# Reordering the work of the two mixing slots in a fused attention and spectral-mix kernel

## The chip, the cores and the metric

The kernel runs on one core of a Trainium2 chip. The metric is the device time of one execution in microseconds (us). The kernel before took 959.21 us (median of 3 runs, 957.13 to 961.86).

## The reference

Soft-capped attention over 8 batches, 12 heads, 448 positions and head size 64 gives x; a mixing layer works on it:

```
scores = cap * tanh((q @ k.T / 8) / cap)
x      = softmax(scores) @ v                     # heads joined: 448 x 768 per batch
theta  = x @ w_theta
y      = w_tok_r @ (x * cos(theta)) + w_tok_i @ (x * sin(theta))
u      = x + y
out    = u + max(u @ w_ch, 0)
```

All arrays are float32. The kernel computes the mixing products from two rounded parts of each operand, a high one and a low one, with three matmuls per product (high by high, low by high, high by low).

## The kernel before, in words

The work is cut into 48 slots (`slot`, and `opening` for the first eight), one for each pair of heads. A slot s computes the scores of its pair in two halves (words SA and SB of the scripts below, PE line L214), their tanh (ACT L216) and exponential (A and B, ACT L222), and for the pair before it the product with v (V, PE L254), its copy out of PSUM (x, ACT L260) and the row sums of the exponentials by matmuls with ones (r, PE L273). From slot 8 on each slot also carries a sixth of one batch's mixing layer. The six parts of a batch are: three blocks of theta (th0 to th2), three more (th3 to th5), three blocks of the token mixing (mix0 to mix2), three more (mix3 to mix5), and twice three blocks of the channel product (ch). A part's matmuls fill most of PE's slot: 54 for three th or ch, 63 for three mix. "The first mixing slot" is below the one with mix0 to mix2, "the second" the one with mix3 to mix5.

Between th and mix each of the six blocks j passes through these steps, by their words in the scripts:

- fold (DVE L344 to L346): theta is brought into one turn; sincos (ACT L350, L351): the sine and cosine of three blocks at once, with a load of ACT's table before it and another before the next tanh.
- rotate (DVE L355) and turn: a transpose within 32 by 32 squares (DVE L362), then a store of 448 KB to a scratch buffer in DRAM (SP queue, L364).
- back: four DMAs that read the block back in its other order (SP queue, L370). They wait until the store has landed.
- high (ACT L378) and low (DVE L384): the two rounded parts, zh and zl. Each of the two tiles has two buffers, so that high2 and low2 wait until mix0 is done, high5 and low5 until mix3 is done.
- mix (PE L392 to L394), gain (DVE L398, which adds the result to x and frees its PSUM buffer), us (ACT L318 and DVE L319, the parts of u), ch, and the evacuation of ch (DVE L406).

Nothing reorders this work: each engine and each DMA queue does its instructions in the order in which the scripts name the steps. `part_scripts` has one script for each of the six parts, `TAIL` the scripts of the last slots, in which no attention is left (batch 7, and the last part of batch 6). The SP queue carries also the loads of q and k (word q, L182: slot s loads for slot s+2 into a buffer that prep, DVE L192 and L193, must have read before), the four DMAs that spread the reciprocal row sums (inv: DVE L300, then L304), the output stores (L407) and the weight loads (L107). The loads of v go through ACT's queue (L186).

The weights are split into high and low parts on the chip (`Split`) at the places listed in `WEIGHTS`: ">" loads a block, "*" scales it on ACT (L111) and "#" on DVE (L114), and the bare name does the split, five to six instructions on DVE (L119 to L128); where `act` is true the rounding among them is ACT's (L124). Channel blocks ch2 to ch5 are loaded and split in slots 10 to 13, beside the mixing of batch 0. Even blocks use one staging buffer and odd ones another, the same two (`g_sb`) that hold the angles of blocks 0 to 2 and 3 to 5.

PSUM accumulators come from a pool of four buffers in turn. A matmul group can start only when its buffer's last reader is done: the copy x, the reciprocal, the gain or L406.

## Time and profile before

| | before |
|---|---|
| time, median of 3 runs | 959.21 us |
| the profiled execution's own time | 966.61 us |
| its span, from the first to the last instruction | 964.8 us |
| PE busy | 924.9 us (96%) |
| DVE busy | 688.4 us (71%) |
| ACT busy | 588.8 us (61%) |
| mean granted TensorE clock over the span | 0.983 |

Durations below come from the profiled execution. The ends of matmuls are modelled, so a row of busy PE hides nothing but also says little; the number to read is the distance from one matmul's start to the next one's, and windows that are cut at the start of a group of matmuls give it.

### The profile page before, as it was taken

The page shows a single profiled execution, that of the slowest core. Times are in us where ns is not written, and L with a number is a line of the kernel's source. Part 1 is how long each engine was busy: PE and PEld are TensorE (multiplying, and loading weights), DVE is VectorE, ACT ScalarE, POOL GpSimd, SP SyncE. Part 2 cuts the span into 40 slices and gives each one's busy share as a digit, 9 for nine tenths or more (in the row PEclk, how much of TensorE's full clock was granted, in tenths as well). Part 3 has the DMA queues.
Part 4 walks back from the last instruction along what each step waited for, and adds up shares of the span by engine and source line. Part 5 has one row for each costly group of instructions (what it writes and reads, how often), then busy time and mean ns, then how long its engine had stood idle before and what let it go on. Part 6 is the DMA issues. An engine that isn't in the chain of part 4 may idle for free. (4 is left out here: it accounts for less than half of the span.)

```text
span 964.8 us, 12481 instructions
## 1 busy us (share of the span) xinstructions
PE 924.9 (96%) x4888; PEld 668.0 (69%) x4888; DVE 688.4 (71%) x877; ACT 588.8 (61%) x561; POOL 0.4 (0%) x6
## 2 busy tenths in 40 slices
PE   8999988989989999999998999899999999999797
PEld 4334656657767787677676767676876677789697
DVE  5998975887876578666777568775787568775641
ACT  6988864467844687555956469445874568644220
POOL 0000000000000000000000000000000000000000
PEclk9999989999999999999999999999999999999899
DMA  7674155422552235432542324622254333411701
GB/s 242 198 222 116 61 148 158 144 80 72 156 163 77 75 106 149 113 112 68 153 144 62 102 67 144 181 67 77 83 156 134 86 96 119 149 38 49 238 2 60
DMA packets 65154, 112.64 MB, mean 117 GB/s; under 512 B 8128, under 2 KB 44992, under 8 KB 65088
## 3 DMA queue, kind: packets, MB, share of 16 engines
q1 hardware_dynamic: 60096, 102.82, 35.4%
q10 hardware_dynamic: 4992, 8.95, 3.2%
q8 instruction: 40, 0.66, 0.3%
q14 instruction: 26, 0.21, 0.1%
HBM read 67.70 MB, written 33.03 MB: 104 GB/s over the span
## 5 line engine op out<-in xcount | busy, mean ns | idle before, releaser
L216 ACT ACTIVATE p<-s,qscale 112x1792 f32<-112x1792 f32 x96 | 168.5, 1755 | 140.1 <-PE s L214 139.9
L222 ACT ACTIVATE p<-p,cap_sb 112x1792 f32<-112x1792 f32 x96 | 169.4, 1785 | 0.4
L254 PE MATMUL a<-p,v 112*64 112x448 f32 x768 | 154.9, 545 | 0.0
L392 PE MATMUL mx<-wtk_h,zh 128*128 128x448 f32 x336 | 128.5, 383 | 12.7 <-ACT zh L378 12.7
L394 PE MATMUL mx<-wtk_h,zl 128*128 128x448 f32 x336 | 127.5, 380 | 8.3 <-DVE zl L384 8.2
L393 PE MATMUL mx<-wtk_l,zh 128*128 128x448 f32 x336 | 126.1, 375 | 0.0
L254 PEld LDWEIGHTS a<-p,v 112*64 112x64 f32 x768 | 50.8, 136 | 86.9 <-issue 76.8
L327 PE MATMUL ch<-us,wch_h 128*128 128x448 f32 x288 | 107.1, 372 | 0.0
L327 PE MATMUL th<-xs,wth_h 128*128 128x448 f32 x288 | 106.9, 371 | 0.0
L328 PE MATMUL ch<-us,wch_h 128*128 128x448 f32 x288 | 105.4, 366 | 0.0
L328 PE MATMUL th<-xs,wth_h 128*128 128x448 f32 x288 | 105.3, 366 | 0.0
L329 PE MATMUL ch<-us,wch_l 128*128 128x448 f32 x288 | 105.3, 366 | 0.0
L329 PE MATMUL th<-xs,wth_l 128*128 128x448 f32 x288 | 105.3, 366 | 0.0
L384 DVE TENSOR_TENSOR zl<-g_sb,zh 128x896 fp32r<-128x896 f32 x48 | 51.9, 1083 | 70.7 <-ACT zh L378 70.5
L247 DVE TENSOR_TENSOR ps<-ps,p 112x896 f32<-112x896 f32 x80 | 87.1, 1089 | 1.4
L392 PEld LDWEIGHTS mx<-wtk_h,zh 128*128 128x128 f32 x336 | 65.5, 195 | 26.2 <-ACT zh L378 14.9
L378 ACT CAST zh<-g_sb 128x896 fp32r<-128x896 f32 x48 | 44.9, 937 | 63.2 <-DMA g_sb<-turn 31.4
L300 DVE RECIPROCAL ri<-r 128x448 f32<-128x448 f32 x24 | 70.6, 2944 | 16.6 <-PE r L273 16.6
L394 PEld LDWEIGHTS mx<-wtk_h,zl 128*128 128x128 f32 x336 | 65.4, 195 | 18.0 <-DVE zl L384 12.3
L393 PEld LDWEIGHTS mx<-wtk_l,zh 128*128 128x128 f32 x336 | 65.5, 195 | 5.5
L406 DVE SCALAR_TENSOR_TENSOR x<-ch,x 128x448 f32<-128x448 f32 x48 | 29.6, 619 | 50.2 <-PE ch L329 50.2
L327 PEld LDWEIGHTS ch<-us,wch_h 128*128 128x128 f32 x288 | 54.2, 188 | 10.3 <-issue 2.7
(73 smaller groups left out, 1338.5 us busy)
## 6 DMA issues: line engine op xcount, KB each, us to landing
turn<-g_sb SPq DMA_DIRECT2D x48, 448.0 KB, 2.8
g_sb<-turn SPq DMA_DIRECT2D x192, 112.0 KB, 3.2
qk_sb<-in_qk SPq DMA_DIRECT2D x35, 448.0 KB, 3.9
bc<-ri SPq DMA_DIRECT2D x96, 112.0 KB, 2.3
out_dram<-x SPq DMA_DIRECT2D x48, 224.0 KB, 2.0
v<-in_v ACTq DMA_DIRECT2D x39, 224.0 KB, 2.6
qk<-in_qk SPq DMA_DIRECT2D x13, 448.0 KB, 3.5
g_sb<-in_wth SPq DMA_DIRECT2D x6, 768.0 KB, 5.3
```

The source lines that it names most:

```text
L216: return lambda: nc.scalar.activation(pp, sp[:CP, :, :, :S], AF.Tanh, scale=qscale[:CP])
L222: nc.scalar.activation(pp, pp, AF.Exp, scale=cap_sb[:CP])
L247: nc.vector.tensor_tensor(pst[k], pst[k], pt[k, 1][:, i], op=ALU.add)
L254: nc.tensor.matmul(acc[hh * D : (hh + 1) * D, :S], va[:, hh, c, :], pt[k, c // 2][:, c % 2, hh, :], start=c == 0, stop=c == NCH - 1)
L300: nc.vector.reciprocal(ri, r[:, :S])
L327: nc.tensor.matmul(acc[:, :S], wh[:, j, ms], t[:, 0, :], start=j == 0, stop=False)
L328: nc.tensor.matmul(acc[:, :S], wh[:, j, ms], t[:, 1, :], start=False, stop=False)
L329: nc.tensor.matmul(acc[:, :S], wl[:, j, ms], t[:, 0, :], start=False, stop=j == NJ - 1)
L384: nc.vector.tensor_tensor(zl.rearrange("p c (g t) -> p c g t", g=4), turned(j), zh.bitcast(F32).rearrange("p c (g t) -> p c g t", g=4), op ...
L392: nc.tensor.matmul(acc[:, :S], zh[:, c, :], wtk_h[:, c, :], start=c == 0, stop=False)
L393: nc.tensor.matmul(acc[:, :S], zh[:, c, :], wtk_l[:, c, :], start=False, stop=False)
L394: nc.tensor.matmul(acc[:, :S], zl[:, c, :], wtk_h[:, c, :], start=False, stop=c == NC2 - 1)
```

## The change

Four scripts and the weight list are written in another order; no computation is added or dropped. In the first mixing slot: high1 moves ahead of the sines, low0 and low1 follow at once on DVE, the load q moves from behind the fourth back to just behind prep, rotate5, turn5 and back5 move in from the second mixing slot, back4 and back5 now stand ahead of inv (whose four DMAs go out on the same queue), and gain1 moves in from the second slot. In the slot before it, b (DVE L247, the sum over the second half of the exponentials) moves ahead of fold5. In the tail high0, low0, high1 and low1 move from behind the three ch blocks to around the second sincos. In the weight list ch4 is scaled and rounded on DVE instead of ACT, and the load of ch3 is issued ahead of the split of ch2, where it stood behind the load of ch4.

```diff
-            steps["ch", m] = Split(room_g(m), w_ch[m], wch_h[:, :, ms], wch_l[:, :, ms], m != 2)
+            steps["ch", m] = Split(room_g(m), w_ch[m], wch_h[:, :, ms], wch_l[:, :, ms], m not in (2, 4))
...
-        (8, "b"): "tk5", (8, "c"): "*tk6 *ch1", (9, "a"): "tk6 ch1", (10, "c"): ">ch2", (11, "c"): "#ch2 ch2 >ch4 >ch3", (12, "b"): "*ch3 ch3 >ch5", (12, "c"): "*ch4 ch4", (13, "b"): "*ch5 ch5",
+        (8, "b"): "tk5", (8, "c"): "*tk6 *ch1", (9, "a"): "tk6 ch1", (10, "c"): ">ch2", (11, "c"): ">ch3 #ch2 ch2 >ch4", (12, "b"): "*ch3 ch3 >ch5", (12, "c"): "#ch4 ch4", (13, "b"): "*ch5 ch5",
...
-            " A th3 fold3 a B th4 fold4 back2 wc th5 fold5 b",
-            "SA high0 sincos1 low0 V wa x v r high1 low1 SB tB prep wb rotate3 turn3 high2 mix0 gain0 low2 rotate4 turn4 back3 inv A"
-            " back4 q B wc mix1 mix2",
-            "SA gain1 a- gain2 rotate5 turn5 high3 low3 V wa x v r high4 low4 SB tB prep b- back5 q wb A mix3 a high5 low5 gain3 us0"
+            " A th3 fold3 a B th4 fold4 back2 wc th5 b fold5",
+            "SA high0 low0 high1 sincos1 low1 V wa x v r SB tB prep q wb rotate3 turn3 high2 rotate4 turn4 back3 mix0 gain0 low2"
+            " rotate5 turn5 back4 back5 inv A B wc mix1 gain1 mix2",
+            "SA a- gain2 high3 low3 V wa x v r high4 low4 SB tB prep b- q wb A mix3 a high5 low5 gain3 us0"
...
-        "rotate0 turn0 rotate1 turn1 back0 rotate2 turn2 back1 th3 fold3 th4 fold4 back2 th5 fold5 sincos1 rotate3 turn3 rotate4 turn4"
+        "rotate0 turn0 rotate1 turn1 back0 rotate2 turn2 back1 th3 fold3 th4 fold4 back2 th5 fold5 high0 low0 sincos1 high1 low1 rotate3 turn3 rotate4 turn4"
...
-        "high0 low0 high1 low1 mix0 high2 low2 gain0 us0 mix1 high3 low3 gain1 us1 mix2 high4 low4 gain2 us2",
+        "mix0 high2 low2 gain0 us0 mix1 high3 low3 gain1 us1 mix2 high4 low4 gain2 us2",
```

The SP queue in the two mixing slots of batch 2, from the return of block 2 on, before (turn_j is block j's scratch buffer, bc a spread reciprocal):

```order
L370 DMA g_sb_87<-turn_2_2532 32x4x224 x4
L364 DMA turn_3_2685<-g_sb_88 128x896
L364 DMA turn_4_2716<-g_sb_88 128x896
L370 DMA g_sb_88<-turn_3_2685 32x4x224 x4
L304 DMA bc_2724<-ri_2722 64x448 x2
L304 DMA bc_2727<-ri_2722 64x448 x2
L370 DMA g_sb_88<-turn_4_2716 32x4x224 x4
L182 DMA qk_sb<-in_qk 128x896
L364 DMA turn_5_2802<-g_sb_88 128x896
L370 DMA g_sb_88<-turn_5_2802 32x4x224 x4
L182 DMA qk_sb<-in_qk 128x896
```

The same stretch of the SP queue after the change:

```order
L370 DMA g_sb_87<-turn_2_2532 32x4x224 x4
L182 DMA qk_sb<-in_qk 128x896
L364 DMA turn_3_2686<-g_sb_88 128x896
L364 DMA turn_4_2692<-g_sb_88 128x896
L370 DMA g_sb_88<-turn_3_2686 32x4x224 x4
L364 DMA turn_5_2725<-g_sb_88 128x896
L370 DMA g_sb_88<-turn_4_2692 32x4x224 x4
L370 DMA g_sb_88<-turn_5_2725 32x4x224 x4
L304 DMA bc_2737<-ri_2735 64x448 x2
L304 DMA bc_2740<-ri_2735 64x448 x2
L182 DMA qk_sb<-in_qk 128x896
```

The store and the return of block 5 now stand ahead of the reciprocals' DMAs, and no load of q and k stands directly ahead of that store; one stands directly ahead of block 3's store instead.

DVE in the first mixing slot of batch 1 before (zl_j is the low part of block j, mx_j a mixing result, the pair L355 and L362 a rotate and its transpose):

```order
L384 TENSOR_TENSOR zl_1_1779<-g_sb_87,zh_1_1777 128x896
L192 CAST hi_1796<-qk_sb 128x896
L193 TENSOR_TENSOR lo_1797<-qk_sb,hi_1796 128x896
L355 TENSOR_TENSOR g_sb_88<-g_sb_88,x_915 128x896
L362 STREAM_TRANSPOSE g_sb_88<-g_sb_88 128x896
L398 TENSOR_TENSOR x_564<-mx_0_1806,x_564 128x448
L384 TENSOR_TENSOR zl_2_1829<-g_sb_87,zh_2_1804 128x896
L355 TENSOR_TENSOR g_sb_88<-g_sb_88,x_1063 128x896
L362 STREAM_TRANSPOSE g_sb_88<-g_sb_88 128x896
L300 RECIPROCAL ri_1839<-r_1772 128x448
L398 TENSOR_TENSOR x_628<-mx_1_1854,x_628 128x448
```

DVE at the same place after the change:

```order
L384 TENSOR_TENSOR zl_1_1761<-g_sb_87,zh_1_1757 128x896
L192 CAST hi_1796<-qk_sb 128x896
L193 TENSOR_TENSOR lo_1797<-qk_sb,hi_1796 128x896
L355 TENSOR_TENSOR g_sb_88<-g_sb_88,x_919 128x896
L362 STREAM_TRANSPOSE g_sb_88<-g_sb_88 128x896
L355 TENSOR_TENSOR g_sb_88<-g_sb_88,x_1067 128x896
L362 STREAM_TRANSPOSE g_sb_88<-g_sb_88 128x896
L398 TENSOR_TENSOR x_564<-mx_0_1815,x_564 128x448
L384 TENSOR_TENSOR zl_2_1838<-g_sb_87,zh_2_1805 128x896
L355 TENSOR_TENSOR g_sb_88<-g_sb_88,x_1200 128x896
L362 STREAM_TRANSPOSE g_sb_88<-g_sb_88 128x896
L300 RECIPROCAL ri_1852<-r_1776 128x448
```

The second rotate and transpose stand ahead of zl_2, and the third pair has come in ahead of the reciprocal.

## Rows read from the trace of the kernel before

**Rows 1.** The page, its first line on the engines: busy time, share of the span, instructions.

```profile
PE 924.9 (96%) x4888; PEld 668.0 (69%) x4888; DVE 688.4 (71%) x877; ACT 588.8 (61%) x561; POOL 0.4 (0%) x6
```

**Rows 2.** What PE waited for over the whole span: line waited for, us in total, times, the longest.

```profile
PE mx L392 <- ACT zh L378: 12.7, 6, 2.9
PE s L214 <- ACT p L216: 9.2, 9, 4.2
PE mx L394 <- DVE zl L384: 8.2, 8, 5.4
```

**Rows 3.** Windows over the 63 matmuls of the second mixing slot, each from the first matmul's start to the start of the group behind it, for batches 0, 2 and 6, and the sum over the seven windows of batches 0 to 6: length, busy us of PE, PEld, DVE, ACT and POOL with instructions, granted TensorE clock (PEclk), busy share of the DMA engines, GB/s.

```profile
151.59:169.64 18.05, 14.99 (x66) 12.62 (x64) 10.57 (x13) 8.30 (x8) 0.00 (x0) 0.91 0.47 148
...
388.55:404.06 15.51, 13.59 (x67) 11.60 (x65) 11.09 (x13) 8.30 (x8) 0.00 (x0) 1.00 0.46 140
...
842.94:855.99 13.05, 13.05 (x66) 11.76 (x64) 10.17 (x13) 8.31 (x8) 0.00 (x0) 1.00 0.24 76
sum 116.79, PE 101.17 PEld 85.91 DVE 80.55 ACT 58.11 POOL 0.00; mean PE 14.45 PEld 12.27 DVE 11.51 ACT 8.30 POOL 0.00
```

**Rows 4.** The timeline of PE in batch 2: the first matmul of mix0, and the first of mix5 with the idle time ahead of it and what ended that. Columns: start, us, engine, line, operation, tiles, shape, count.

```profile
369.52 0.47 PE L392 MATMUL mx<-wtk_h,zh 128*128 128x448 f32 x1
...
398.87 0.47 PE L392 MATMUL mx<-wtk_h,zh 128*128 128x448 f32 x1 [1.47 <-ACT zh L378]
```

**Rows 5.** ACT in batch 2: the sine, the tanh of the second mixing slot, high5.

```profile
369.00 1.31 ACT L351 ACTIVATE g_sb<-g_sb 128x1344 f32<-128x1344 f32 x1
384.09 1.75 ACT L216 ACTIVATE p<-s,qscale 112x1792 f32<-112x1792 f32 x1 [5.25 <-PE s L214]
397.87 0.94 ACT L378 CAST zh<-g_sb 128x896 fp32r<-128x896 f32 x1 [2.82 <-DVE ps L244]
```

**Rows 6.** DMA issues on the SP queue in batch 2, KB each and us from issue to landing: block 5's store (issued at 388.06), block 4's store (380.19), the four returns of block 5 (from 394.03), a load of q and k with nothing ahead of it (338.08).

```profile
turn<-g_sb SPq DMA_DIRECT2D x1, 448.0 KB, 6.0
turn<-g_sb SPq DMA_DIRECT2D x1, 448.0 KB, 2.8
g_sb<-turn SPq DMA_DIRECT2D x4, 112.0 KB, 2.4
qk_sb<-in_qk SPq DMA_DIRECT2D x1, 448.0 KB, 3.4
```

**Rows 7.** The SP queue in the timeline of batch 2: start and length of the issues.

```profile
388.06 0.38 SPq L364 DMA_DIRECT2D turn<-g_sb  x1
394.03 1.74 SPq L370 DMA_DIRECT2D g_sb<-turn  x4
```

**Rows 8.** DVE in batch 2: low1, rotate3, the transpose of block 5.

```profile
371.60 1.09 DVE L384 TENSOR_TENSOR zl<-g_sb,zh 128x896 fp32r<-128x896 f32 x1 [3.43 <-ACT zh L378]
374.27 1.08 DVE L355 TENSOR_TENSOR g_sb<-g_sb,x 128x896 f32<-128x896 f32 x1
386.05 1.11 DVE L362 STREAM_TRANSPOSE g_sb<-g_sb 128x896 f32<-128x896 f32 x1
```

**Rows 9.** Windows with the columns of rows 3. In order: the row sums, SB and the mixing in the first mixing slot of batch 0 (8 + 8 + 63 matmuls); row sums, SB and three ch (8 + 8 + 54); SA, v, SB and three ch in slot 13 (8 + 16 + 8 + 54); the same counts with three th in slot 9; the 126 mixing matmuls of batch 7; the 108 th matmuls of batch 7; the row sums of a first mixing slot (batch 2, 8 matmuls); the row sums of the slot behind the second (batch 2, 8 matmuls).

```profile
122.92:145.05 22.13, 19.52 (x81) 13.72 (x79) 15.77 (x16) 12.78 (x11) 0.00 (x0) 0.85 0.48 134
174.49:188.28 13.79, 13.79 (x73) 10.86 (x71) 10.98 (x14) 7.14 (x9) 0.00 (x0) 1.00 0.63 198
188.28:211.91 23.63, 19.44 (x88) 12.92 (x88) 21.59 (x28) 14.25 (x14) 0.00 (x0) 0.93 0.34 111
100.32:118.08 17.76, 17.76 (x88) 12.40 (x87) 17.18 (x26) 15.46 (x15) 0.00 (x0) 1.00 0.13 44
904.20:937.47 33.27, 27.89 (x127) 25.23 (x126) 17.08 (x23) 6.62 (x9) 0.00 (x0) 0.90 0.32 103
871.14:893.18 22.04, 22.04 (x109) 20.28 (x108) 11.91 (x20) 9.42 (x13) 0.00 (x0) 1.00 0.09 37
366.84:368.11 1.27, 1.27 (x12) 0.29 (x10) 1.27 (x2) 1.26 (x2) 0.00 (x0) 1.00 0.94 200
408.62:409.51 0.89, 0.89 (x10) 0.16 (x9) 0.00 (x0) 0.77 (x2) 0.00 (x0) 1.00 0.00 0
```

**Rows 10.** Batch 0: the start of fold5 and the sums of b on DVE in the first mixing slot; the landing of the four returns of block 1 (issued from 120.49; columns of rows 6); ACT's scaling of ch3 and the tanh of slot 13.

```profile
122.83 0.62 DVE L344 SCALAR_TENSOR_TENSOR g_sb<-g_sb 128x448 f32<-128x448 f32 x1
...
124.22 2.21 DVE L247 TENSOR_TENSOR ps<-ps,p 112x896 f32<-112x896 f32 x2
...
g_sb<-turn SPq DMA_DIRECT2D x4, 112.0 KB, 3.8
...
183.21 0.91 ACT L111 ACTIVATE g_sb<-g_sb 128x768 f32<-128x768 f32 x1 [3.94 <-DMA g_sb<-in_wch]
195.58 1.75 ACT L216 ACTIVATE p<-s,qscale 112x1792 f32<-112x1792 f32 x1
```

**Rows 11.** DVE's windows over two splits, with the columns of rows 3: ch2 (scaled and rounded on DVE) and ch3 (scaled and rounded on ACT).

```profile
169.21:175.32 6.11, 6.11 (x35) 1.98 (x33) 5.90 (x9) 2.47 (x3) 0.00 (x0) 1.00 0.00 0
184.15:189.07 4.92, 4.92 (x25) 3.98 (x25) 4.78 (x6) 3.33 (x3) 0.00 (x0) 1.00 0.46 129
```

**Rows 12.** Batch 7: the cosine on ACT, the three evacuations of ch on DVE, the third matmul of mix0 on PE.

```profile
898.38 1.42 ACT L350 ACTIVATE g_sb<-g_sb,quarter 128x1344 f32<-128x1344 f32 x1 [3.85 <-DVE g_sb L346]
907.45 1.65 DVE L406 SCALAR_TENSOR_TENSOR x<-ch,x 128x448 f32<-128x448 f32 x3
910.14 0.74 PE L394 MATMUL mx<-wtk_h,zl 128*128 128x448 f32 x1 [5.38 <-DVE zl L384]
```

## The prediction

> **What bounds the kernel now.** I read the line of the engines first, then PE's waits, then windows cut at the starts of matmul groups, and last the timelines of the engines around the gaps.
>
> PE is busy for 924.9 of 964.8 us [rows 1], so its own instruction stream sets the time and only what holds that stream up can be won. The waits name it: mixing matmuls that wait for zh on ACT and for zl on DVE, and scores that wait for a tanh [rows 2]. These rows alone understate the price. The windows show the whole of it: the 63 matmuls of the second mixing slot take 13.05 us in batch 6, 15.51 in batch 2 and 18.05 in batch 0, and 116.79 over batches 0 to 6 [rows 3]. Seven times 13.05 is 91.35, so 25.4 us are lost there, all in batches 0 to 5. Part is waiting and part is clock: in batch 0 the granted clock over the window is 0.91, which is (1 - 0.91) x 18.05 = 1.6 us lost at 1.2 instead of 2.4 GHz, while batch 2, with its idle 1.47 us ahead of mix5 [rows 4], kept 1.00 [rows 3].
>
> What ends that wait? high5 starts at 397.87 [rows 5], after block 5's returns, issued from 394.03 to 395.77 and landed 2.4 us later [rows 6, 7]. They waited for block 5's store, issued at 388.06 and landed 6.0 us later, where block 4's took 2.8 [rows 6, 7]. The store had stood on the SP queue behind a load of q and k. Batch 6 is a natural experiment: no pair is left to load for, and its window has no loss at all [rows 3].
>
> Three more places lose time. Batch 0's first mixing slot takes 22.13 us where its matmuls need 13.79 + 9 x 0.204 = 15.6 (108 in 22.04 us is 0.204 each): 6.5 lost, with a mean clock of 0.85 [rows 9]. Slot 13 takes 23.63 where slot 9 takes 17.76: 5.9 lost [rows 9]. Batch 7's mixing takes 33.27 where 126 x 0.204 = 25.7 would do: 7.6 lost [rows 9]. And the row sums of a first mixing slot take 1.27 us where others take 0.89 [rows 9].
>
> **The second mixing slot, batches 0 to 5.** I replay batch 2 with the rows' durations. In the new order high1 (0.94 us, as high5) stands ahead of the sines, which end at 369.00 + 1.31 + 0.9 = 371.2 [rows 5]. DVE no longer idles 3.43 us for high1 [rows 8]: low1 is out of the way, prep starts when the scores are through, at mix0's start (369.5) [rows 4], and ends near 371.3. So rotate3 starts at 371.3 instead of 374.27 [rows 8]. Two pairs of rotate and transpose take 4 x 1.1 = 4.3, the gain and low2 1.6 (low2 1.09, as low1), and the third pair 2.2 [rows 8]: low2 ends at 377.2 and the transpose of block 5 at 379.4, where it ended at 386.05 + 1.11 = 387.2 [rows 8]. mix2 wants low2's result at 369.52 + 44 x 0.207 = 378.6 (0.207 is 13.05 over 63) [rows 3, 4]: 1.4 us of slack.
>
> On the SP queue the load of q and k goes out at 371.3 and block 3's store at 373.5; block 5's store at 379.4 lands after 2.8 us, at 382.2, its returns take 1.74 to issue and 2.4 to land [rows 6, 7]: 386.3. high5 can't start before mix3 frees its buffer at 388.55 + 21 x 0.207 = 392.9 [rows 3]. So the wait for the DMA is gone, and what is late next is DVE: after low4 near 389.8 come prep, b's two sums and the first sum of the slot's own pair, 1.7 + 2.2 + 1.1, then low5, 1.1 [rows 8, 10], which ends near 395.9. mix5 wants it at 388.55 + 44 x 0.207 = 397.7. Nothing is left on PE: -25.4 us, between -16 (a third stays) and -25.4.
>
> Moving b ahead of fold5 takes the wait out of the row sums: 6 x (1.27 - 0.89) = -2.3 us in batches 1 to 6 [rows 9].
>
> The load of q and k is the part that could bite. Block 5's store behind such a load took 6.0 us, 3.2 more than block 4's [rows 6]; a load alone takes 3.4 [rows 6]. The Trainium skill ("DMA: Bandwidth & Descriptors", section "Queues, rings and completion order") says that on each DMA engine the descriptors of one issuing engine are consumed in ring order. By that rule the load, which goes out 2.2 us ahead of block 3's store, could delay it by up to 3.2 us, and its return from near 380 to near 383. The trace agrees with the rule as far as the 6.0 goes. By the row as by the rule the sum stays, since high3 follows the tanh of 384.09 + 1.75 = 385.8 [rows 5]; but half the slack is used, and I give the second rival below a little more for it.
>
> **Batch 0's first mixing slot.** The row sums wait for b's sums, which come 124.22 - 122.83 = 1.4 us earlier [rows 10], at 125.0. The second half of the row sums would start at 122.92 + 0.45 without a wait [rows 9], so 1.7 us of wait stay. A gap of 1.47 us left the clock alone in batch 2, longer ones didn't always [rows 3, 4]; I add 1.0 for half a chance of about 2 us at half clock. Here high1 also waits for block 1's returns, which land 3.8 us after issue, the last near 126.2 [rows 10]; ACT stands still for them, sines, tanh and low2 shift, and mix2 waits some 0.9 us. In all 6.5 - 1.7 - 1.0 - 0.9 = 2.9 us won, between 0 and 6.5.
>
> **The channel weights.** Slot 13 loses because ACT's scaling of ch3 waits for its load until 183.21, with the exponentials, ch4's scaling and then the tanh of 195.58 queued behind it [rows 10], and PE waits for that tanh. The load now goes out as soon as low5 has read the buffer, ahead of ch2's split instead of behind it, and ACT has nothing to do for ch4. DVE pays 6.11 - 4.92 = 1.2 us more for ch4 [rows 11]. Does it keep up? Counted from mix3's first matmul, DVE reaches ch2's split at 11.3 (low5 ends at 6.5, and two gains, three us and b's sums follow, 4.8) and then has the splits of ch2 to ch5, 6.1 + 4.9 + 6.1 + 4.9 [rows 11], and some 14 us of other work without a pause: 47. PE without waits reaches ch5 at 13.05 + 4.9 (SA and v) + 13.79 + 17.76 - 3.7 (ch5 itself) = 45.8 [rows 3, 9]. So about 1 us of wait is new there. 5.9 - 1.0 = 4.9 won, between 1 and 5.9.
>
> **Batch 7.** mix0 no longer waits for low0. But low1 now stands ahead of rotate3, and high1 (0.94) and low1 (1.09) both run after the sines, so that the rotates end 1.9 us later and with them the evacuations of ch3 to ch5, from 907.45 on [rows 12]. mix1's accumulator is the one that the first of them frees, at 907.45 + 0.55 + 1.9 = 909.9; mix1 could start at 904.2 + 21 x 0.204 = 908.5 [rows 9]. So 1.4 us of wait takes the place of 5.4 [rows 12]; with 1.0 for the clock 7.6 - 1.4 - 1.0 = 5.2 are won, between 3 and 7.6.
>
> **The sum.** 25.4 + 2.3 + 2.9 + 4.9 + 5.2 = 40.7 us off the profiled execution's 966.61: 925.9. The median of the runs is 7.4 us below that execution. If this is a fixed surplus, the median becomes 959.2 - 40.7 = 918.5; if the profile lengthens just those waits that now go, it becomes 925.9. I take the middle, 922.
>
> **The rivals.**
> - *A new wait in the first mixing slot.* high1 ahead of the sines, or the load ahead of block 3's store, makes low2 late and mix2 waits in each batch. For it: only 1.4 us of slack. Against it: high1's own wait is short, as block 1's returns have landed by then in batch 2. At 1.5 us and a half-clock stretch of 1.6 in six batches it costs 18: 940.
> - *DVE takes over at the edges.* Batch 0, slot 13 and batch 7 win nothing, because DVE has no pause there. That takes back 13: 935.
> - *The change doesn't do what it says.* mix5 keeps waiting, for low5 behind DVE's sums instead of for the DMA, so that block 5's earlier return is worth nothing and 25.4 us come back: 947. Against it stands batch 6, whose DVE did the same work but for one prep, without a wait. Together with the rival before it this would be no change: 960.
> - *Slower.* high1 holds ACT until block 1's returns have landed, and each us beyond the slack is paid by the tanh, DVE's chain and PE in every batch. To eat 40.7 us and 5 more in seven batches it has to be 6.5 us per batch beyond the slack of 1.4, so that the returns would land some 8 us later than the 3.8 measured [rows 10]: 965.
>
> **How the numbers follow.** Forecast 65%, first rival 13%, second 14%, third 3%, second and third together 3%, slower 2%. The forecast's own range goes from 912 (all 47.7 us of the four places and the row sums won, on the lower reading of the median) to 930 (the upper reading, and 4 us of the terms at their worse ends). To take in the second rival the range is 912 to 935; the first and the third lie above it. About 0.5% (5 us) is what a measurement of this kernel can tell from no change: faster 65 + 13 + 14 + 3 = 95%, within it 3%, slower 2%.
>
> **What would show it.** Right: seven windows of the second mixing slot near 13.05 us; rotate3 about 3 us earlier against mix0; block 5's store landing in under 4 us; a short wait at mix1 in batch 7 that ends with L406; no wait for ACT's tanh in slot 13; the clock at 1.00 but for batch 0 and the edges. Wrong: waits of mix2 for zl in the first mixing slot, or mix5 still waiting, then for zl alone.

## The result, and the profile after

The changed kernel took 923.45 us (median of 4 runs, 922.08 to 925.17), the kernel before beside it 960.54 (4 runs, 957.13 to 964.27). The ratio is 0.9614, with a 95% interval of 0.9572 to 0.9656: faster by 3.9%, near the forecast of 922 and inside its range.

The profiled execution of the changed kernel took 922.08 us. Its span is 920.3 us at a mean granted clock of 0.999, where before it was 964.8 at 0.983. The line of the engines on its page, which answers to [rows 1]:

```profile
PE 904.7 (98%) x4888; PEld 659.2 (72%) x4888; DVE 689.3 (75%) x879; ACT 587.8 (64%) x559; POOL 0.4 (0%) x6
```

The engines do the same work in a span that is 44.5 us shorter. PE's busy time fell by 20.2 us though no matmul went. Part of that is clock, since a matmul at half clock is busy for longer. Part is waiting that the modelled ends count as busy: the row sums' 1.27 us of [rows 9] were all busy at a clock of 1.00, and they are 0.89 now. The clock's share can be bounded by the means: (1 - 0.983) x 964.8 = 16.4 us of full clock were missing before, (1 - 0.999) x 920.3 = 0.9 are missing now. So by that column up to 15.5 of the 44.5 us are clock that was kept, and the rest is in the main waiting that is gone.

What PE waits for after the change: line waited for, us in total, times, the longest. Beside [rows 2]:

```profile
PE s L214 <- ACT p L216: 5.2, 9, 1.9
PE mx L392 <- DVE x L406: 1.4, 1, 1.4
PE r L273 <- DVE ps L247: 1.3, 1, 1.3
...
PE ch L329 <- DVE wch_l L128: 0.9, 1, 0.9
```

The waits of mixing matmuls for zh (12.7 us) and for zl (8.2) have left the list. The three short lines that stand in it now are the three that the working had announced: batch 7's mix1, batch 0's row sums and ch5.

Windows over the 63 matmuls of the second mixing slot, cut and with columns as in [rows 3], for batches 0, 2 and 6 and the sum over batches 0 to 6; behind them the same for the first mixing slot, batches 0 and 2 and the sum:

```profile
145.41:158.45 13.04, 13.04 (x66) 11.76 (x64) 11.86 (x15) 7.46 (x7) 0.00 (x0) 1.00 0.51 182
...
366.58:379.63 13.05, 13.05 (x66) 11.76 (x65) 12.65 (x16) 7.58 (x8) 0.00 (x0) 1.00 0.18 56
...
804.45:817.49 13.04, 13.04 (x65) 11.75 (x63) 11.30 (x14) 7.55 (x8) 0.00 (x0) 1.00 0.01 1
sum 91.31, PE 91.31 PEld 82.28 DVE 86.44 ACT 52.90 POOL 0.00; mean PE 13.04 PEld 11.75 DVE 12.35 ACT 7.56 POOL 0.00
...
125.50:138.87 13.37, 13.30 (x65) 11.68 (x63) 10.64 (x10) 11.01 (x9) 0.00 (x0) 1.00 0.67 199
...
347.55:360.59 13.04, 13.04 (x65) 11.75 (x63) 12.61 (x12) 9.67 (x8) 0.00 (x0) 1.00 0.56 182
...
sum 91.65, PE 91.58 PEld 82.21 DVE 85.03 ACT 70.36 POOL 0.00; mean PE 13.08 PEld 11.74 DVE 12.15 ACT 10.05 POOL 0.00
```

All seven second slots now have batch 6's length of before, 13.05 us. The first slots did not pay for it. In batch 2 DVE is busy for 12.65 of the 13.05 us where it was for 11.09 of 15.51 [rows 3]: the wait is gone and the slack behind it nearly too.

The edges after the change: windows with the columns of [rows 9], of batch 0's row sums, SB and mixing; of SB and three ch in slot 13 (without the SA and v that [rows 9] has in its window); of the 126 mixing matmuls of batch 7; of the row sums of batch 2's first mixing slot:

```profile
120.74:138.87 18.13, 16.80 (x81) 12.59 (x79) 15.30 (x17) 13.13 (x11) 0.00 (x0) 1.00 0.74 211
...
181.93:195.95 14.02, 13.17 (x64) 10.62 (x62) 13.67 (x19) 9.38 (x10) 0.00 (x0) 1.00 0.31 98
...
865.70:893.01 27.31, 25.91 (x127) 23.58 (x126) 16.84 (x22) 6.60 (x9) 0.00 (x0) 1.00 0.39 127
...
345.24:346.13 0.89, 0.89 (x10) 0.16 (x8) 0.89 (x2) 0.87 (x2) 0.00 (x0) 1.00 1.00 189
```

Set group against group, the distances between the starts of PE's matmul groups in the two traces differ as follows (all other groups agree within 0.12 us):

| place | before to after, us | forecast |
|---|---|---|
| second mixing slots, batches 0 to 5 | -25.5 | -25.4 |
| row sums, batches 1 to 6 (6 x 0.38) | -2.3 | -2.3 |
| batch 0: row sums -2.1, SB -1.6, mixing -0.3 | -4.0 | -2.9 |
| slot 13: v -4.3, SB -1.4, ch +0.9 | -4.8 | -4.9 |
| batch 7's mixing | -6.0 | -5.2 |
| opening: warm-up matmuls -0.6, first scores -1.6 | -2.1 | none |
| sum | -44.5 (rounded terms add to -44.7) | -40.7 |

The opening's 2.1 us are not the change's, as the last section shows. The change itself is worth 42.4 us between these two executions, and 3.0 of them, in batch 0, are a stretch at half clock that the same code up to that place does not bring in every execution (run 7).

### The profile page after: what moved, and what is told of

Its sections match the earlier page's. It is cut to its first block, busy times and chain, and to the rows that moved or that the text cites. A ratio compares the mean times of both kernels' runs of the same rounds, so it can differ in the third digit from the quotient of the medians.

```text
span 920.3 us, 12487 instructions
## 1 busy us (share of the span) xinstructions
PE 904.7 (98%) x4888; PEld 659.2 (72%) x4888; DVE 689.3 (75%) x879; ACT 587.8 (64%) x559; POOL 0.4 (0%) x6
## 4 chain that ended last, share of the span: by engine, by line
PE 87%; DVE 7%; ACT 3%; issue 1%; DMA 1%; SPq 0%; DVEq 0%; ACTq 0%
PE a L254 14%; PE s L214 14%; PE mx L392 7%; PE mx L394 7%; PE mx L393 7%; PE th L327 6%; PE th L328 6%; PE th L329 6%; PE ch L327 6%; PE ch L329 6%; PE ch L328 6%; PE r L273 2%; ACT p L216 2%; DVE ri L300 1%; DVE g_sb L355 1%
## 5 line engine op out<-in xcount | busy, mean ns | idle before, releaser
L392 PE MATMUL mx<-wtk_h,zh 128*128 128x448 f32 x336 | 124.5, 370 | 1.4 <-DVE x L406 1.4
L394 PE MATMUL mx<-wtk_h,zl 128*128 128x448 f32 x336 | 123.0, 366 | 0.1
L393 PE MATMUL mx<-wtk_l,zh 128*128 128x448 f32 x336 | 122.9, 366 | 0.0
L247 DVE TENSOR_TENSOR ps<-ps,p 112x896 f32<-112x896 f32 x80 | 87.0, 1088 | 1.4
L300 DVE RECIPROCAL ri<-r 128x448 f32<-128x448 f32 x24 | 70.7, 2944 | 16.4 <-PE r L273 16.4
L384 DVE TENSOR_TENSOR zl<-g_sb,zh 128x896 fp32r<-128x896 f32 x48 | 51.7, 1086 | 29.5 <-ACT zh L378 25.7
L392 PEld LDWEIGHTS mx<-wtk_h,zh 128*128 128x128 f32 x336 | 63.1, 188 | 12.1 <-issue 3.9
L394 PEld LDWEIGHTS mx<-wtk_h,zl 128*128 128x128 f32 x336 | 63.1, 188 | 5.9 <-DVE zl L384 0.5
L406 DVE SCALAR_TENSOR_TENSOR x<-ch,x 128x448 f32<-128x448 f32 x48 | 29.6, 620 | 50.2 <-PE ch L329 50.2
L393 PEld LDWEIGHTS mx<-wtk_l,zh 128*128 128x128 f32 x336 | 63.1, 188 | 5.2
L327 PEld LDWEIGHTS th<-xs,wth_h 128*128 128x128 f32 x288 | 54.1, 188 | 9.6 <-issue 5.2
```

Of the source, the lines that this page charges most:

```text
L247: nc.vector.tensor_tensor(pst[k], pst[k], pt[k, 1][:, i], op=ALU.add)
L300: nc.vector.reciprocal(ri, r[:, :S])
L327: nc.tensor.matmul(acc[:, :S], wh[:, j, ms], t[:, 0, :], start=j == 0, stop=False)
L392: nc.tensor.matmul(acc[:, :S], zh[:, c, :], wtk_h[:, c, :], start=c == 0, stop=False)
L393: nc.tensor.matmul(acc[:, :S], zh[:, c, :], wtk_l[:, c, :], start=False, stop=False)
L394: nc.tensor.matmul(acc[:, :S], zl[:, c, :], wtk_h[:, c, :], start=False, stop=c == NC2 - 1)
```

## The experiments

Runs 1 to 4 stood beside a run of the kernel before of 964.83 us, runs 5 to 7 beside one of 961.99; each of these seven times is of one execution. Executions of the kernel before lay up to 9.5 us apart (957.13 to 966.61) and those of the changed one 3, so the verdicts rest on the windows of the stage concerned, cut as above.

| kernel | time, us | second mixing slots 0 to 6 | first mixing slots 0 to 6 | batch 7's mixing |
|---|---|---|---|---|
| before | 966.61 | 116.8 | 91.9 | 33.3 |
| changed | 922.08 | 91.3 | 91.7 | 27.3 |
| 1: before, third rotation early | 968.21 | 121.6 | 91.3 | 34.0 |
| 2: before, load early | 948.71 | 101.2 | 91.3 | 33.2 |
| 3: changed, load back | 924.28 | 93.6 | 91.5 | 27.6 |
| 4: changed, sines first | 940.95 | 91.3 | 110.6 | 27.3 |
| 5: changed, tail of before | 929.13 | 91.3 | 91.9 | 34.1 |

### 1. The third rotation early, alone

```diff
-            "SA high0 sincos1 low0 V wa x v r high1 low1 SB tB prep wb rotate3 turn3 high2 mix0 gain0 low2 rotate4 turn4 back3 inv A"
-            " back4 q B wc mix1 mix2",
-            "SA gain1 a- gain2 rotate5 turn5 high3 low3 V wa x v r high4 low4 SB tB prep b- back5 q wb A mix3 a high5 low5 gain3 us0"
+            "SA high0 sincos1 low0 V wa x v r high1 low1 SB tB prep wb rotate3 turn3 high2 mix0 gain0 low2 rotate4 turn4 back3 rotate5 turn5 inv A"
+            " back4 back5 q B wc mix1 mix2",
+            "SA gain1 a- gain2 high3 low3 V wa x v r high4 low4 SB tB prep b- q wb A mix3 a high5 low5 gain3 us0"
```

> The kernel before with one part of the change alone: rotate5, turn5 and back5 in the first mixing slot (ahead of inv, and behind back4). The sines still stand ahead of high1, and the load q stays behind the returns. Theory (block 5 was late by its own place on DVE and by the load ahead of its store): the waits ahead of mix5 go, and the seven windows of the second mixing slot sum to about 91 to 92 us instead of 116.8. But without high1 ahead of the sines DVE has no room for the third pair: the reciprocal ends near 385.2 by batch 2's clock of before, 1.2 us after the next product with v (384.0) wants its PSUM buffer, so that this product's 3.16 us grow to about 4.4 in batches 0 to 6. In all some 943 us. Rival (only the load ahead of the store made it late): the windows would gain nothing from the new place as such, since the load no longer stands between either way; it can't be told apart here by the windows, but the rival sees no new wait and gives 935.

968.21 us: a miss. The second mixing slots got worse, 121.6 us for 116.8 (all but batch 0's, 13.58 for 18.05), and the wait of the product with v that was expected beside them did not come; that part of the theory falls. Batch 2's second mixing slot in this kernel, and then what ACT, DVE and SP do there (timelines; start, length, instruction, idle time ahead and what ended it):

```profile
380.93:399.79 18.86, 15.37 (x66) 12.81 (x64) 12.53 (x16) 8.19 (x8) 0.00 (x0) 0.91 0.40 113
```

```profile
385.18 0.94 ACT L378 CAST zh<-g_sb 128x896 fp32r<-128x896 f32 x1 [5.01 <-DMA g_sb<-turn]
```

```profile
388.24 0.63 DVE L192 CAST hi<-qk_sb 128x896 fp32r<-128x896 f32 x1 [1.00 <-DMA qk_sb<-in_qk]
```

```profile
377.54 2.39 SPq L304 DMA_DIRECT2D bc<-ri  x4
379.97 3.99 SPq L370 DMA_DIRECT2D g_sb<-turn  x8
384.00 6.37 SPq L182 DMA_DIRECT2D qk_sb<-in_qk  x2
```

Read SP's rows first. The returns of block 4 stand behind the reciprocals' four DMAs, which end on the queue at 379.9, an us before mix3 starts at 380.93; high4 idles 5.01 us for them. The load of q and k stands behind all eight returns, so prep waits for it, and low5 is behind prep on DVE. By this reading the rotation moved up was worth nothing in batches 1 to 6 because the returns stood behind DMAs that wait for a reciprocal. No run moves the returns alone, and how much of the slot's loss is high4's and how much prep's was not separated.

### 2. The load early, alone

```diff
-            "SA high0 sincos1 low0 V wa x v r high1 low1 SB tB prep wb rotate3 turn3 high2 mix0 gain0 low2 rotate4 turn4 back3 inv A"
-            " back4 q B wc mix1 mix2",
+            "SA high0 sincos1 low0 V wa x v r high1 low1 SB tB prep q wb rotate3 turn3 high2 mix0 gain0 low2 rotate4 turn4 back3 inv A"
+            " back4 B wc mix1 mix2",
```

> The kernel before with one part alone: the load of q and k (word q of the first mixing slot) moved to just behind prep; rotate5, turn5, back5 and the sines stay. Theory (both causes count): block 5's store lands in about 3 us instead of 6.0, but it is still issued near 388 by batch 2's clock, its returns land near 395.3, and low5 follows the first sum of the slot's own pair and ends near 398.8, about 1.1 us too late for mix5. In batch 0 the weight load of ch2 still stands ahead of the store and the wait stays. The seven windows sum to about 102 (before 116.8, all waits gone 91.4). Rival (the load alone was the cause): 91 to 96, with batch 0 alone over 13.3. Rival (the place on DVE alone): 110 or more.

948.71 us, and the second mixing slots take 101.2, as expected: the load alone brings 15.6 of the 25.5 us. One part was a miss: batch 0's slot lost most of its excess too (14.86 us for 18.05). Batches 0, 2 and 6 and the sum; then the matmul of mix5 that waits now:

```profile
148.42:163.28 14.86, 13.57 (x65) 11.60 (x63) 9.45 (x11) 8.30 (x8) 0.00 (x0) 1.00 0.48 154
...
379.33:394.17 14.84, 13.57 (x65) 11.60 (x64) 10.91 (x13) 8.31 (x8) 0.00 (x0) 1.00 0.38 115
...
825.16:838.20 13.04, 13.04 (x65) 11.75 (x63) 10.16 (x13) 8.31 (x8) 0.00 (x0) 1.00 0.25 79
sum 101.17, PE 94.22 PEld 81.42 DVE 74.26 ACT 58.15 POOL 0.00; mean PE 13.46 PEld 11.63 DVE 10.61 ACT 8.31 POOL 0.00
```

```profile
390.10 0.48 PE L394 MATMUL mx<-wtk_h,zl 128*128 128x448 f32 x1 [1.26 <-DVE zl L384]
```

The clock is at 1.00 in every one of them. In batch 2, which had kept its clock before [rows 3], the gain is only 15.51 - 14.84 = 0.7 us; in batch 0, which had not, it is 3.2. Batches 0, 1, 4 and 5 had a clock of 0.90 or 0.91 over windows of 17.12 to 18.35 us before, which is 6.6 us of full clock lost in all. So some 6.6 of the 15.6 us are clock that no longer falls, and the rest is shorter waiting. 9.8 us (101.2 - 91.35) of waiting stay. In batch 2 the DMA is no longer what holds mix5: high5 ends at 387.82, and low5 starts at 388.96, right behind the sums on DVE.

Block 5's store also corrects a reason of the prediction, which had laid all of its 3.2 us of delay on the load. Its landing, first in this kernel's batch 5 with the load of v that goes out 0.3 us ahead of it on ACT's queue, then in this kernel's batch 6, where no load is left to make (KB each, us from issue to landing):

```profile
turn<-g_sb SPq DMA_DIRECT2D x1, 448.0 KB, 4.3
v<-in_v ACTq DMA_DIRECT2D x1, 224.0 KB, 3.5
```

```profile
turn<-g_sb SPq DMA_DIRECT2D x1, 448.0 KB, 3.1
```

In batches 1 to 5 the store took 5.3 to 6.1 us in the kernel before, behind both loads, and 4.0 to 4.9 here, behind v alone. The load of q and k, 0.5 us ahead of it (1.5 in batch 4), thus cost it 1.0 to 1.9 us, batch against batch. The load of v, by the distance to batch 6's 3.1, cost it some 0.9 to 1.8; that part is inferred, since no run moves the load of v. The Trainium skill ("DMA: Bandwidth & Descriptors", section "Queues, rings and completion order") says that on each DMA engine the descriptors of a ring are consumed in order. The first part agrees with it; that rule speaks of one ring, and v goes out on another.

### 3. The changed kernel with the load behind the returns and the reciprocals

```diff
-            "SA high0 low0 high1 sincos1 low1 V wa x v r SB tB prep q wb rotate3 turn3 high2 rotate4 turn4 back3 mix0 gain0 low2"
-            " rotate5 turn5 back4 back5 inv A B wc mix1 gain1 mix2",
+            "SA high0 low0 high1 sincos1 low1 V wa x v r SB tB prep wb rotate3 turn3 high2 rotate4 turn4 back3 mix0 gain0 low2"
+            " rotate5 turn5 back4 back5 inv A q B wc mix1 gain1 mix2",
```

> The changed kernel with one part undone: the load of q and k in the first mixing slot stands behind the returns and the reciprocals' DMAs again. Theory: with block 5's store ahead of it the load is off the path; the seven windows stay at 13.05 each, block 3's store lands in 2.5 us instead of 4.2, the time is that of the changed kernel (922 to 925). Rival (the load's place is a part of the gain): prep of the second slot waits for the load, low5 gets late behind it and mix5 waits 1 us or more in six batches: 930 or more.

924.28 us, a time that the theory had allowed, but its windows did not come out as it said. Five of the seven second slots stay at 13.05 us, batches 3 and 4 take 14.24 and 14.11, since prep waits 2.95 and 2.83 us there for the late load (0.67 to 1.29 us in batches 1, 2 and 5). The rival's six waits came in two batches. In batch 3:

```profile
475.67:489.91 14.24, 13.30 (x65) 11.67 (x63) 11.00 (x13) 7.57 (x8) 0.00 (x0) 1.00 0.32 96
```

```profile
479.90 0.63 DVE L192 CAST hi<-qk_sb 128x896 fp32r<-128x896 f32 x1 [2.95 <-DMA qk_sb<-in_qk]
```

So the early load is worth 2.3 us with the rest of the change in place, and 15.6 without it: the parts of the gain overlap and can't be added. The run also settles the cost that the prediction feared of the load ahead of block 3's store. That store takes the same with the load 2.5 to 3.2 us ahead of it (changed kernel) as without (this one): 2.5 us in batches 1, 3, 4 and 5 of both. The row, alike for both kernels:

```profile
turn<-g_sb SPq DMA_DIRECT2D x1, 448.0 KB, 2.5
```

In batch 2 it took 4.2 in both, so that this delay is not the load's either. The prediction had allowed up to 3.2 us. At this distance the measurement is none: the load itself takes 3.0 to 3.3 us from issue to landing there, so that it is over, or nearly, when the store goes out.

### 4. The changed kernel with the sines ahead of high1 and low1

```diff
-            "SA high0 low0 high1 sincos1 low1 V wa x v r SB tB prep q wb rotate3 turn3 high2 rotate4 turn4 back3 mix0 gain0 low2"
+            "SA high0 sincos1 low0 V wa x v r high1 low1 SB tB prep q wb rotate3 turn3 high2 rotate4 turn4 back3 mix0 gain0 low2"
```

> The changed kernel with one part undone: the sines stand ahead of high1 and low1 again in the first mixing slot. Theory: rotate3 starts about 3 us later against mix0, low2 ends about 1.5 us after mix2 wants it, and mix2 waits 1.5 to 2 us in each of seven batches, some with a stretch at half clock: 934 to 940. The windows of the second mixing slot stay at 13.05. Rival (the order of sines and roundings only fills idle time): no wait of mix2, 922 to 925.

940.95 us, as the theory had it. The order of high1 and the sines carries the first mixing slot: without it the three rotations make low2 late, and mix2 waits in every batch. PE's wait, then the windows of batches 1 and 2 and the sum of the seven:

```profile
PE mx L394 <- DVE zl L384: 11.3, 7, 1.8
```

```profile
238.36:255.02 16.66, 14.85 (x65) 12.97 (x64) 14.06 (x14) 9.67 (x8) 0.00 (x0) 0.90 0.48 159
351.43:366.56 15.13, 13.31 (x66) 11.68 (x65) 12.52 (x12) 9.68 (x8) 0.00 (x0) 1.00 0.48 153
...
sum 110.62, PE 99.32 PEld 86.92 DVE 92.17 ACT 67.99 POOL 0.00; mean PE 14.19 PEld 12.42 DVE 13.17 ACT 9.71 POOL 0.00
```

This is the first rival come true: 19.0 us more over the seven slots (110.6 - 91.65), where the rival had been priced at 18. In the changed kernel low2 ends at 354.39 + 1.07 = 355.46 in batch 2, and mix2's first matmul that reads it, the 45th of the slot, starts near 347.55 + 44 x 0.207 = 356.66: the slack that keeps this out is 1.2 us.

### 5 to 7. The edges put back one by one

Run 5, the tail's order:

```diff
-        "rotate0 turn0 rotate1 turn1 back0 rotate2 turn2 back1 th3 fold3 th4 fold4 back2 th5 fold5 high0 low0 sincos1 high1 low1 rotate3 turn3 rotate4 turn4"
+        "rotate0 turn0 rotate1 turn1 back0 rotate2 turn2 back1 th3 fold3 th4 fold4 back2 th5 fold5 sincos1 rotate3 turn3 rotate4 turn4"
...
-        "mix0 high2 low2 gain0 us0 mix1 high3 low3 gain1 us1 mix2 high4 low4 gain2 us2",
+        "high0 low0 high1 low1 mix0 high2 low2 gain0 us0 mix1 high3 low3 gain1 us1 mix2 high4 low4 gain2 us2",
```

> The changed kernel with the tail's part undone: high0, low0, high1 and low1 of batch 7 behind the three ch blocks again. Theory: mix0 waits again for low0 behind rotates and evacuations, and batch 7's 126 mixing matmuls take about 33 us instead of 27.3: 928 to 929. Rival (the wait of mix1 for L406 was as dear as the one that went): under 29, and no more than 2 us on the time.

929.13 us, as expected, and batch 7's mixing takes 34.06 us, where it was 33.27 before:

```profile
865.97:900.03 34.06, 28.68 (x127) 25.90 (x126) 17.10 (x23) 6.61 (x9) 0.00 (x0) 0.90 0.32 102
```

Run 6, the weight list (with ch4 rounded on ACT again):

```diff
-            steps["ch", m] = Split(room_g(m), w_ch[m], wch_h[:, :, ms], wch_l[:, :, ms], m not in (2, 4))
+            steps["ch", m] = Split(room_g(m), w_ch[m], wch_h[:, :, ms], wch_l[:, :, ms], m != 2)
...
-        (8, "b"): "tk5", (8, "c"): "*tk6 *ch1", (9, "a"): "tk6 ch1", (10, "c"): ">ch2", (11, "c"): ">ch3 #ch2 ch2 >ch4", (12, "b"): "*ch3 ch3 >ch5", (12, "c"): "#ch4 ch4", (13, "b"): "*ch5 ch5",
+        (8, "b"): "tk5", (8, "c"): "*tk6 *ch1", (9, "a"): "tk6 ch1", (10, "c"): ">ch2", (11, "c"): "#ch2 ch2 >ch4 >ch3", (12, "b"): "*ch3 ch3 >ch5", (12, "c"): "*ch4 ch4", (13, "b"): "*ch5 ch5",
```

> The changed kernel with the weight list's part undone: ch3's load behind ch4's and behind the split of ch2, ch4 scaled and rounded on ACT. Theory: ACT's scaling of ch3 waits for its load, and the tanh of slot 13 behind it is late again. Since PE now arrives 5 us earlier there than in the kernel before, the wait is at least as long as before (4.3 us and a stretch at half clock) and up to 9 us: 928 to 934. Rival (that wait only followed from the late second mixing slot of batch 0): under 1.5 us, 923 to 924.

925.41 us: less than expected. Slot 13 loses 2.3 in v and 1.3 in SB and wins 0.8 in ch, 2.8 us in all where 4.8 had come back with the whole change. The scaling of ch3 on ACT waits 2.21 us for its load, not 3.94 [rows 10]:

```profile
170.51 0.92 ACT L111 ACTIVATE g_sb<-g_sb 128x768 f32<-128x768 f32 x1 [2.21 <-DMA g_sb<-in_wch]
```

The load stands behind ch2's split, and DVE comes to that split sooner: 11.3 us after mix3's first matmul, where it was 17.6 before. A shorter mixing slot is not enough for that. In runs 1 and 2, which have the old list and a shorter slot in batch 0, the split starts at 14.2 and 15.6 us, and slot 13 (v, SB and ch) is 0.9 us shorter and 0.9 longer than before. So 2.8 of slot 13's 4.8 us belong to the weight list, and 2.0 came with the rest of the change, which the runs do not divide further.

Run 7, b behind fold5:

```diff
-            " A th3 fold3 a B th4 fold4 back2 wc th5 b fold5",
+            " A th3 fold3 a B th4 fold4 back2 wc th5 fold5 b",
```

> The changed kernel with one part undone: b behind fold5 again in the slot ahead of the first mixing slot. Theory: the row sums of the first mixing slot take 1.27 us again instead of 0.89 in batches 1 to 6 (2.3 us), and in batch 0 they wait 1.4 us longer, perhaps with a stretch at half clock: 3.7 to 7 us in all, 926 to 930. Rival: the wait is hidden elsewhere and the time stays within 1 us.

930.63 us, at the upper end. The groups put 2.3 us on the row sums of batches 1 to 6 (6 x 0.38), 4.1 on batch 0, and 2.3 on the opening, which is not this edit's. Batch 0's window stands beside the 18.13 above, the wait of its row sums beside the 1.3:

```profile
123.05:145.25 22.20, 19.59 (x82) 13.78 (x80) 17.88 (x18) 12.85 (x11) 0.00 (x0) 0.85 0.68 199
```

```profile
PE r L273 <- DVE ps L247: 2.6, 1, 2.6
```

But this one word does not hold all of batch 0's 4.0 us. Runs 1 and 2 have b behind fold5 too, and the same wait of 2.6 us, and there the clock stayed at 1.00. Their windows take 19.18 and 19.16 us; run 1's:

```profile
122.63:141.81 19.18, 16.56 (x81) 12.68 (x79) 15.86 (x16) 12.83 (x11) 0.00 (x0) 1.00 0.53 158
```

Where the clock stays, the changed kernel's 18.13 us are thus 1.0 us shorter. The other 3.0 are a stretch at half clock (0.50 over SB in both), which followed that wait in two of four traces: this one and the kernel before. The shorter wait of 1.2 to 1.3 us left the clock at 1.00 in all six traces with the new order.

### 8. A version with the edges mended

Three of the waits that the change left, each taken on: b one step further up in batch 0, the wait that ch5 has for DVE, and in the tail the rotation that makes L406 late.

```diff
-            " A th3 fold3 a B th4 fold4 back2 wc th5 b fold5",
+            " A th3 fold3 a B th4 b fold4 back2 wc th5 fold5",
...
-            "SA V wa x v r norm inv SB tB prep q wb A ch3 a B ch4 b wc ch5",
+            "SA V wa x v r norm inv SB tB wb prep q A ch3 a B ch4 b wc ch5",
...
-        " back3 rotate5 turn5 back4 back5",
+        " back3 back4",
...
-        "mix0 high2 low2 gain0 us0 mix1 high3 low3 gain1 us1 mix2 high4 low4 gain2 us2",
+        "rotate5 turn5 back5 mix0 high2 low2 gain0 us0 mix1 high3 low3 gain1 us1 mix2 high4 low4 gain2 us2",
```

> The changed kernel with its last three waits taken aim at: b right behind the first exponential sum, ahead of fold4; the split of ch5 ahead of prep in slot 13; rotate5, turn5 and back5 of batch 7 behind the evacuations of ch3 to ch5. Theory: batch 0's row sums no longer wait (2.2 us), ch5 no longer waits for its low weights (0.9), mix1 of batch 7 no longer waits for L406 (1.6): 4 to 5 us under the changed kernel beside it, 918 to 920. Rival (each wait is followed by another just behind it, DVE being late as a whole at these places): 1.5 us or less.

The changed kernel ran again beside it:

> The changed kernel once more, on the same chip, as the yardstick: 922 to 925 us.

922.06 us (median of 5 runs, 921.68 to 922.60), against 924.32 (5 runs, 923.78 to 924.67) for the changed kernel and 959.21 for the kernel before (9 runs): ratios to the latter of 0.9612 (0.9590 to 0.9635) and 0.9633 (0.9611 to 0.9655). It is the best of the versions, by 2.3 us, and less than was expected. PE's waits, and batch 7's window:

```profile
PE mx L394 <- DVE zl L384: 1.0, 2, 0.5
```

```profile
867.00:892.69 25.69, 25.69 (x128) 23.67 (x127) 16.81 (x22) 6.51 (x9) 0.00 (x0) 1.00 0.41 135
```

Batch 7 now takes 126 x 0.204 = 25.7 us, with no loss (-1.9), and ch5's wait is gone (-1.1). In batch 0 the row sums win 1.2, but mix0 and mix2 wait 0.54 and 0.44 us for zl instead, and its mixing takes 1.5 more. PE comes to the mixing sooner, and the rest does not follow. low0 stands on DVE behind the folds that b overtook. The sines stand on ACT behind high1, which waits 2.87 us for block 1's returns, and DVE idles ahead of rotate3 until they are done:

```profile
131.29 1.09 DVE L355 TENSOR_TENSOR g_sb<-g_sb,x 128x896 f32<-128x896 f32 x1 [2.41 <-ACT g_sb L351]
```

So in this slot moving a step of DVE up only moves the wait.

## Why the prediction came out, point by point

**The second mixing slots (25.4 forecast, 25.5 measured).** The mechanism was right. The replay of batch 2 can be laid on the trace, with 369.52 - 347.55 = 21.97 us taken off its times (mix0's start before and after):

| step, us | replay, shifted | measured |
|---|---|---|
| rotate3 starts | 349.3 | 349.60 |
| low2 ends | 355.2 | 355.46 |
| transpose of block 5 ends | 357.4 | 357.61 |
| its store lands | 360.2 | 361.3 |
| high5 starts | 370.9 | 370.96 |
| low5 ends | 373.9 | 373.66 |

The rows of the trace after, DVE, SP and ACT in turn:

```profile
349.60 1.09 DVE L355 TENSOR_TENSOR g_sb<-g_sb,x 128x896 f32<-128x896 f32 x1 [0.19 <-ACT g_sb L351]
...
354.39 1.07 DVE L384 TENSOR_TENSOR zl<-g_sb,zh 128x896 fp32r<-128x896 f32 x1
...
356.50 1.11 DVE L362 STREAM_TRANSPOSE g_sb<-g_sb 128x896 f32<-128x896 f32 x1
...
372.58 1.08 DVE L384 TENSOR_TENSOR zl<-g_sb,zh 128x896 fp32r<-128x896 f32 x1
```

```profile
357.93 0.38 SPq L364 DMA_DIRECT2D turn<-g_sb  x1
358.41 4.64 SPq L370 DMA_DIRECT2D g_sb<-turn  x8
```

```profile
370.96 0.94 ACT L378 CAST zh<-g_sb 128x896 fp32r<-128x896 f32 x1 [0.82 <-PE mx L393]
```

high5 now waits for a matmul to free its buffer and no longer for a DMA, as the working said. Only the store was off: it was issued behind block 3's returns and took 3.4 us, not 2.8. The landings of that store and of its returns (KB each, us from issue):

```profile
turn<-g_sb SPq DMA_DIRECT2D x1, 448.0 KB, 3.4
```

```profile
g_sb<-turn SPq DMA_DIRECT2D x4, 112.0 KB, 2.6
```

The last return goes out by 358.41 + 4.64 = 363.05 and lands 2.6 us later, at 365.7: 5.3 us of room ahead of high5 covered the delay. What the replay did not see is how the gain is made up. By runs 1 and 2 neither the load nor the rotation brings the 25 us by itself, and by run 3 all but 2.3 of them come without the load's new place.

**The row sums (2.3).** Right to the digit in the trace, and run 7 takes it back.

**Batch 0 (2.9 forecast, 4.0 measured).** The term was too small, and its parts were off in both directions. The 15.6 us that the slot's matmuls were said to need took row sums at their later length of 0.89 us; in slot 8 they need 1.82, as run 8 shows, where no wait is left in them:

```profile
123.20:125.02 1.82, 1.82 (x10) 0.29 (x8) 1.79 (x3) 0.29 (x1) 0.00 (x0) 1.00 1.10 242
```

The floor is thus 1.82 + 1.69 + 13.05 = 16.56 us, the loss before was 22.13 - 16.56 = 5.6 and not 6.5, and after it is 18.13 - 16.56 = 1.57: the 1.26 us that stayed at the row sums (1.7 had been worked out) and 0.33 at mix2 (0.9 had). The 1.0 us laid aside for the clock was not needed; the window's clock is 1.00. The wrong floor thus made the term 0.9 too large, and the three allowances made it 2.0 too small. And 3.0 us of the loss before were the stretch at half clock that runs 1 and 2 did not have: set against them the gain is 1.0, so that the nearness of 2.9 to 4.0 owes something to luck.

**Slot 13 (4.9 forecast, 4.8 measured).** The size was right and the new wait of "about 1 us" at ch5 is there, 0.85 us. The reason was only in part right: by run 6 the weight list brings 2.8, and the rest of the change the other 2.0. DVE reaches ch2's split 11.3 us after mix3's first matmul in run 6, as the working had counted.

**Batch 7 (5.2 forecast, 6.0 measured).** The wait of mix1 for the first L406 was worked out as 1.4 us and is 1.40; again the 1.0 for the clock was not needed. The two waits, ch5's in slot 13 and mix1's in batch 7:

```profile
192.50 0.47 PE L329 MATMUL ch<-us,wch_l 128*128 128x448 f32 x1 [0.85 <-DVE wch_l L128]
...
871.53 0.44 PE L392 MATMUL mx<-wtk_h,zh 128*128 128x448 f32 x1 [1.40 <-DVE x L406]
```

**From the sum to the median.** This step was the weak one, and two errors met in it. The terms came to 40.7 us and measured 42.4. The profiled execution of before stood 7.4 us above the median, and the two readings of that (a fixed surplus, or a profile that lengthens the waits) were both about the profile; the changed kernel's profiled execution is the lowest of its four, so that there is no fixed surplus. The runs of the kernel before spread over 957 to 967 us and those of the changed one over 922 to 925. Before's profiled execution was a long one of its kind, and what the change took from it, 44.5 us, is more than it took from the median, 960.54 - 923.45 = 37.1. One thing by which executions of that code differ is shown: runs 1 and 2 are the kernel before up to batch 0's mixing, and the stretch at half clock of 3.0 us is missing there (run 7). How much of the 7.4 us it and others like it explain stays open. That the middle of the two readings, 922, came so near the median of 923.45 is luck: neither of the two readings was shown.

**The rivals.** The new wait in the first mixing slot did not come, and run 4 shows that it was close. DVE at the edges cost what the working had, and not the 13 us of the rival. That mix5 keeps waiting is excluded by the windows of the second slots, and that the kernel gets slower by the time.

## What to carry to other kernels

On a queue that works in order, count for each transfer what is directly ahead of it and what that waits for: in run 1 a store moved up was worth nothing while returns stood behind DMAs that wait for another engine, and here a load cost the store behind it 1.0 to 1.9 us at a distance of 0.5 to 1.5 us and nothing at 2.5 to 3.2. Replay one batch with the durations of its own rows, engine by engine, before moving steps; six steps of such a replay came out within 1.1 us here, and it told which engine is late next. And price a wait by the clock behind it too: in run 4 the same 1.8 us of waiting cost 2.1 us or 3.6.

## What the hardware showed that was not expected

**Equal waits, unequal clocks.** In run 4 mix2 waited about 1.8 us in each of batches 1 to 6. In batches 1, 3, 4 and 5 the granted clock over the slot fell to 0.90 and the slot took 16.66 us, in batches 2 and 6 it stayed at 1.00 and the slot took 15.13: the same wait cost 3.6 us or 2.1. The kernel before has the same in its second slots: behind a wait of 2.07 us batch 3 kept 1.00, and behind one of 1.71 batch 5 fell to 0.90. The changed kernel's waits of 0.85 to 1.40 us left the clock alone. So whether a single wait of this size drops the clock is not settled by its length. The Trainium skill ("TensorE: Matmul & The Clock Gate", section "A second HAM failure mode: psum-queue depth-cycling") tells of a kernel in which very short idle times between groups of matmuls come often enough to make the clock go to and fro. These rows agree in that a short wait can do it; here it is one wait in a slot, and not a series.

**The opening differs between executions.** The first eight scores took 3.26 us before and 1.69 after, with identical work. That is not the change's: the trace of the changed kernel that stands beside run 8 has the 3.26 again. Windows of the changed kernel, then of its second trace:

```profile
5.50:7.19 1.69, 1.69 (x9) 0.64 (x8) 0.02 (x1) 0.70 (x1) 0.00 (x0) 1.00 1.03 425
```

```profile
6.44:9.70 3.26, 3.26 (x9) 1.08 (x8) 1.66 (x3) 0.33 (x1) 0.00 (x0) 1.00 1.02 413
```

The clock column reads 1.00 in both and does not tell them apart; 3.26 us is also the length of SB in batch 0 before, where the granted clock from 128.12 to 131.38 is 0.50, against 1.69 at 1.00 after, so that the lower level (1.2 GHz) is the likely reason; why it lasts longer in one execution stays open. A difference of some 2 us between two single executions of this kernel is therefore no evidence on an edit, nor is one of 3 where a stretch like batch 0's has come or gone.
